# Moving output pairs of earlier batches into the load waits at the end of an attention and mixture-of-depths kernel

## The chip, the cores and the metric

The kernel runs on one core of a Trainium2 chip. The metric is the device time of one execution in microseconds; the kernel before takes 269.82 us (median of 3 runs, 269.68 to 270.16). The core has a matrix engine (TensorE, "PE" in the profile, its weight loads "PEld"), a vector engine (VectorE, "DVE"), an activation engine (ScalarE, "ACT"), a general one (GpSimd, "POOL") and one that here only issues stores (SyncE, "SP"). Loads, gathers and scatters are issued from GpSimd's queue, stores from SyncE's, and both are carried by the core's 16 DMA engines.

## The reference

Four batches; each q, k and v has 6208 rows of 256 channels. The attention is over channels: q and k are normalised over the rows, a 256 x 256 matrix is made of them, a softmax is taken along its rows, and v is multiplied by it. Then, in each batch, the 128 rows with the highest gate score go through a two-layer expert and are updated.

```python
def _attn_ref(q, k, v, tau):
    qn = q / (np.linalg.norm(q, axis=1, keepdims=True) + 1e-06)
    kn = k / (np.linalg.norm(k, axis=1, keepdims=True) + 1e-06)
    s = kn.transpose(0, 2, 1) @ qn / tau
    s = s - s.max(-1, keepdims=True)
    a = np.exp(s)
    a /= a.sum(-1, keepdims=True) + 1e-09
    return (v @ a).astype(np.float32)

def _moe_ref(x, w_gate, w1, w2, capacity):      # capacity 128, D 256, F 1024
    scores = np.einsum('bsd,d->bs', x, w_gate)
    out = x.copy()
    for b in range(B):
        top_idx = np.argpartition(-scores[b], capacity)[:capacity]
        xe = x[b, top_idx]
        ye = np.maximum(xe @ w1, 0.0) @ w2
        g = 1.0 / (1.0 + np.exp(-scores[b, top_idx]))
        out[b, top_idx] = x[b, top_idx] + g[:, None] * ye
    return out
```

## The kernel before

Rows are taken in chunks of 1024 (8 rows on each of 128 partitions): 6 full chunks and a remainder of 64 rows. A chunk is handled in two groups of 4 rows, so a batch has 13 groups, listed in `gs`; the last one is the remainder. For each group of v there are up to three kinds of work:

- `T`: 8 transposes of v on TensorE into a PSUM bank, and one copy to SBUF (`vt_sb`), on ScalarE where the flag is 1 and on VectorE where it is 0.
- `S`: gate scores, 8 matmuls that are two columns wide.
- `O`: output, two pairs of four 128x256 matmuls, each pair copied from PSUM to a staging buffer; a whole chunk is stored with one 1 MB transfer.

When all scores of a batch are there, `select_stages` finds the 128 best rows by a seven-step search of the threshold: each step compares and counts on VectorE, sums the counts over partitions with a small matmul, and goes on from the result. Then the rows of v are gathered, go through the expert (`mlp_stages`), and a scatter writes them over the stored rows. The scatter of a batch waits for that batch's stores.

The batches are numbered 0 to 3. In the code `L` is 3, the last one, `E` is 2 and `H` is 1. Batch 2 keeps most of its output (`rest`, from group 4 on) for the end, when there are no loads left. Batch 1 keeps the last chunk of its output, four "late pairs". They can't be written before the scatter, so their updated rows are added in the matmul itself, by one-hot matrices (`late_onehot`) times the expert's result in three bf16 parts:

```python
    def late_pair(k):
        g = late[k // 2]
        onehot, parts = late_moe
        ...
        o_ps = out_psum()
        row = g[1] + k % 2 * 2
        for pj in range(2):
            for cc in range(2):
                nc.tensor.matmul(o_ps[:, pj, :], lhsT=vts[(H, g)][:, cc, k % 2 * 2 + pj, :], rhs=a_sb[:, cc, :],
                                 start=pj == 0 and cc == 0, stop=False)
            for i in range(3):
                nc.tensor.matmul(o_ps[:, pj, :], lhsT=onehot[:, row + pj, :], rhs=parts[:, i, :],
                                 start=False, stop=pj == 1 and i == 2)
        nc.scalar.copy(st[:, row:row + 2, :], o_ps)
```

The plan of the tail, after the last q and k chunk. It stands in TensorE's program order:

```python
    rest = [("O", E, g, False) for g in gs[EARLY:]]        # EARLY = 4
    ...
    T = [("T", L, g, a) for g, a in zip(gs, [1, 1, 1, 0, 1, 1, 0, 1, 0, 1, 0, 1, 0])]
    S = [("S", L, g) for g in gs]
    plan += [("tail",)] + T[:2] + [("late", H, 0)] + T[2:4] + [("adv",), ("a", L)]
    plan += T[4:8] + [("late", H, 1)] + T[8:10] + S[:4] + [("warm", L, 4)] + T[10:] + [("side",)] + S[4:]
```

`("a", L)` finishes the last softmax, `("side",)` finishes the selection of batch 2, and `("warm", L, 4)` and `keep_warm(n)` issue matmuls whose results nobody reads:

```python
    def keep_warm(n):
        bank = ps_o.tile([P, 2, C], F32, name="o_ps")
        for _ in range(n):
            nc.tensor.matmul(bank[:, 0, 0:P], lhsT=ident_b, rhs=ones_b, start=True, stop=True)
```

After the plan, the last batch's selection starts, the stores held back so far ("deferred": 4 chunks) are issued behind the last but one v load, and the output phase follows:

```python
    b = B - 1
    side.append(select_stages(b))
    advance(side)
    advance(side)
    flush_deferred()
    ...
    now[0] = B + 1
    for op in rest:
        do_out(E, op[2], False)
    for i, g in enumerate(gs):
        do_out(b, g, False)
        if i in (8, 9):
            late_pair(i - 6)
    emit_store(H, NFULL - 1)
    while side:
        advance(side)
    while side2:
        advance_all(side2)
    while waiting:
        side2.append(mlp_stages(waiting.pop(0)))
    keep_warm(8)
    while side2:
        advance(side2)
```

In this phase every output pair calls `between()`, which puts the next step of the selection (and later of batch 2's expert) into the program after pairs 2, 4, 6, 8, 10, 13, 15, 18, 20 and so on. So TensorE takes up a step of the search only when it has done the pairs ahead of it:

```python
    def between():
        if now[0] > B:
            pairs[0] += 1
            due = pairs[0] in (2, 4, 6) or pairs[0] > 6 and pairs[0] % 5 in (0, 3)
            if due and not advance(side):
                advance_all(side2)
```

Line numbers that the profile shows: L402 transposes, L409 and L411 their copies, L430 scores, L476 output matmuls, L482 and L484 their copies, L500 and L503 the matmuls of a late pair, L505 its copy, L418 keep_warm, L561 to L636 the selection, L653 to L703 the expert, L535 the stores, L709 the scatter.

Of the kernel before, what the change touches and what calls it, by code (L numbers as in the profile page):

```python
# [26 lines left out]
def kernel(  # L27
# [70 lines left out]
    def groups(ci):  # L98
        return [(ci, 0, 4), (ci, 4, 4)] if ci < NFULL else [(ci, 0, 1)]

    gs = [g for ci in range(NFULL + 1) for g in groups(ci)]
    E = B - 2
    H = B - 3
    late = [(NFULL - 1, 0, 4), (NFULL - 1, 4, 4)]
# [18 lines left out]
    L = B - 1  # L123
    rest = [("O", E, g, False) for g in gs[EARLY:]]
    plan = []
# [17 lines left out]

    T = [("T", L, g, a) for g, a in zip(gs, [1, 1, 1, 0, 1, 1, 0, 1, 0, 1, 0, 1, 0])]
    S = [("S", L, g) for g in gs]
    plan += [("tail",)] + T[:2] + [("late", H, 0)] + T[2:4] + [("adv",), ("a", L)]
    plan += T[4:8] + [("late", H, 1)] + T[8:10] + S[:4] + [("warm", L, 4)] + T[10:] + [("side",)] + S[4:]
    units = []
    for op in plan:
        if op[0] in ("p1", "T"):  # L150
# [222 lines left out]
    side = []  # L373
# [40 lines left out]
# [5 lines that stand above are left out]
# [18 lines left out]
    def out_psum():  # L437

        if now[0] <= B:
            return ps_o.tile([P, 2, C], F32, name="o_ps")  # L440
        turn[0] += 1
        if turn[0] % 4 == 1:
            return ps_s.tile([P, 2, C], F32, name="s_ps")
        if turn[0] % 4 == 3:
            return ps_g.tile([P, 4, P], F32, name="g_ps").rearrange("p a c -> p (a c)").rearrange(
                "p (a c) -> p a c", a=2)
        return ps_o.tile([P, 2, C], F32, name="o_ps")
# [39 lines left out]
# [5 lines that stand above are left out]
        if k == 0:  # L492
            stage_of[(H, NFULL - 1)] = st_pool.tile([P, RPP, C], F32, name="stage")
        st = stage_of[(H, NFULL - 1)]
        a_sb = a_tiles[H][0]
# [10 lines that stand above are left out]
# [27 lines left out]
    def emit_store(b, ci):  # L533
        st = stage_of.pop((b, ci))
        ins = nc.sync.dma_start(out=view(out, b, ci), in_=st if ci < NFULL else st[:REM, 0, :])  # L535
        stores.append((b, ins))
        for o, sca in scatters:
            if o != b:
                tc.declare_no_dep(ins.ins, sca.ins, reason="rows of different batches")
        return ins  # L540
# [253 lines left out]
    def do_out(b, g, scores, defer=False):  # L794
        p2_out(b, g, vts.pop((b, g)), scores)
        if g[1] == 4 or g[0] == NFULL:
            held[b] -= 1
            if defer and now[0] <= B:
                deferred.append((b, g[0]))
            else:  # L800
                emit_store(b, g[0])
        spent((0.21 + (0.05 if scores else 0)) * g[2])
# [41 lines left out]
    while waiting:  # L844
        side2.append(mlp_stages(waiting.pop(0)))
    now[0] = B + 1
    for op in rest:
        do_out(E, op[2], False)
    for i, g in enumerate(gs):
        do_out(b, g, False)  # L850
        if i in (8, 9):
            late_pair(i - 6)
    emit_store(H, NFULL - 1)
    while side:
        advance(side)
# [1 line left out]
        advance_all(side2)  # L857
    while waiting:
        side2.append(mlp_stages(waiting.pop(0)))
    keep_warm(8)  # L860
    while side2:
        advance(side2)

# [34 lines left out]
```

## Time and profile before

| | before |
|---|---|
| time, median of 3 | 269.82 us |
| span of the profiled run | 269.3 us |
| PE busy | 205.6 us (76%) |
| DVE busy | 124.2 us (46%) |
| ACT busy | 80.7 us (30%) |
| bytes moved by DMA | 66.97 MB, mean 249 GB/s |
| stores from SyncE's queue | 24 of 1 MB, 4 of 64 KB |
| last q/k matmul ends | about 202.9 us |
| last v chunk taken up by TensorE | 216.24 us |
| last instruction that a compute engine's queue issues (scatter of batch 3) | 259.75 us |

Times are counted from the span's start. "Busy" is the time in which an engine executes; it says little here, since the kernel passes through stages with different limits. What counts is which wait ends last in the tail, from 203 us on. In rows of single instructions, the numbers are start and length, then engine, line, operation and tiles, and in brackets the idle time just before and what ended it. In the rows of slices, the busy time of each engine is followed by the clock that TensorE was granted (1.00 is full) and the share of time in which the DMA engines were busy.

### The profile page before, as it was taken

The numbers are of one execution on the slowest core, as the hardware profiler recorded it, in microseconds if no ns is written. First come the engines' busy times: TensorE is split into PE (matmuls) and PEld (weight loads), VectorE is DVE, ScalarE is ACT, GpSimd is POOL, SyncE is SP. The second block draws the span as 40 slices with busy tenths as digits, with TensorE's granted clock in tenths as the row PEclk, the third lists the DMA queues.
The fourth block names the chain that finished last, engine by engine and source line by source line (L and its number), as shares of the span: only waits on it lengthen the run. The fifth ranks groups of instructions, "written<-read, shape, count | busy, mean of one in ns | idle before, by whom it ended". The sixth has DMA issues, their size and how long they took to land.

```text
span 269.3 us, 6056 instructions
## 1 busy us (share of the span) xinstructions
PE 205.6 (76%) x2564; PEld 179.6 (67%) x2564; DVE 124.2 (46%) x476; ACT 80.7 (30%) x142; POOL 55.5 (21%) x104
## 2 busy tenths in 40 slices
PE   0197588899936877899978797899998578898820
PEld 0186577789925666789967686889996565587610
DVE  0200003624305376505457957765966537874510
ACT  2102000177710000147702001442107624775410
POOL 7113123211110023313002242211440011011010
PEclk9999899999968799599997999999999955999985
DMA  6999999999999999999999999999999996899960
GB/s 213 232 228 227 212 214 212 215 213 295 317 316 319 277 212 212 214 213 239 317 309 219 211 220 214 212 214 212 212 213 212 209 412 212 369 383 403 377 236 0
DMA packets 17642, 66.97 MB, mean 249 GB/s; under 512 B 2000, under 2 KB 4688, under 8 KB 14544
## 3 DMA queue, kind: packets, MB, share of 16 engines
q0 software_dynamic: 12384, 38.93, 72.4%
q1 hardware_dynamic: 5232, 27.66, 26.2%
q8 instruction: 20, 0.33, 0.4%
q14 instruction: 6, 0.05, 0.0%
HBM read 79.04 MB, written 25.95 MB: 390 GB/s over the span
## 4 chain that ended last, share of the span: by engine, by line
DMA 57%; PE 19%; issue 11%; DVE 7%; POOL 1%; ACT 1%; POOLq 1%; DVEq 0%
DMA k_ch<-in_k_dram 29%; DMA v_ch<-in_v_dram 17%; DMA q_ch<-in_q_dram 8%; PE o_ps L476 5%; PE s_ps L290 2%; DMA out_dram<-stage_rem 2%; PE vt_ps L402 2%; DVE cnt L590 1%; PE sc_ps L430 1%; PE s_ps L476 1%; DVE cmp L586 1%; PE g_ps L294 1%; PE g_ps L292 1%; PE g_ps L476 1%; PE o_ps L686 1%
## 5 line engine op out<-in xcount | busy, mean ns | idle before, releaser
L290 PE MATMUL s_ps<-q_ch,k_ch 128*128 128x256 bf16 x384 | 97.7, 293 | 29.3 <-DMA k_ch<-in_k_dram 28.5
L292 PE MATMUL g_ps<-q_ch 128*128 128x128 bf16 x384 | 89.1, 232 | 1.1 <-DVE nsq L309 1.0
L294 PE MATMUL g_ps<-k_ch 128*128 128x128 bf16 x384 | 89.1, 232 | 0.0
L290 PEld LDWEIGHTS <-k_ch 128*128 128x128 bf16 x384 | 40.3, 105 | 34.8 <-DMA k_ch<-in_k_dram 31.6
L294 PEld LDWEIGHTS <-k_ch 128*128 128x128 bf16 x384 | 40.3, 105 | 8.7 <-issue 1.6
L476 PE MATMUL o_ps<-a_sb,vt_sb 128*128 128x256 bf16 x294 | 44.9, 277 | 1.4 <-ACT vt_sb L409 1.3
L292 PEld LDWEIGHTS <-q_ch 128*128 128x128 bf16 x384 | 40.3, 105 | 1.2 <-issue 0.9
L484 ACT COPY stage<-o_ps 128x512 f32<-128x512 f32 x64 | 36.0, 588 | 16.0 <-PE o_ps L476 15.4
L476 PEld LDWEIGHTS <-vt_sb 128*128 128x128 bf16 (+1 forms) x376 | 30.8, 101 | 8.8 <-issue 3.9
L411 DVE COPY vt_sb<-vt_ps 128x1024 bf16<-128x1024 bf16 (+1 forms) x33 | 20.8, 634 | 32.2 <-PE vt_ps L402 32.1
L402 PEld LDWEIGHTS <-v_ch 128*128 128x128 bf16 x384 | 22.9, 99 | 6.4 <-DMA v_ch<-in_v_dram 5.3
L402 PE MATMUL vt_ps<-ident_b,v_ch 128*128 128x128 bf16 x336 | 24.6, 219 | 2.7 <-DMA v_ch<-in_v_dram 1.9
L430 PEld LDWEIGHTS <-vt_sb 128*128 128x128 bf16 (+1 forms) x376 | 24.0, 98 | 2.5 <-DVE u L553 0.2
L173 POOL DMA_DIRECT2D q_ch<-in_q_dram x23 | 12.7, 553 | 59.2 <-PE g_ps L294 36.3
L430 PE MATMUL sc_ps<-aw_sb,vt_sb 128*128 128x2 bf16 (+1 forms) x376 | 24.3, 164 | 0.0
L305 ACT COPY s_sb<-s_ps 128x512 f32<-128x512 f32 x4 | 2.3, 585 | 72.5 <-PE s_ps L290 42.7
L309 DVE CUSTOM_DVE_ANT_0 junk<-g_ps,ident_f 128x128 f32<-128x128 f32 x16 | 4.7, 291 | 39.1 <-PE g_ps L294 38.7
L173 POOL DMA_DIRECT2D v_ch<-in_v_dram x24 | 12.8, 538 | 24.4 <-DMA k_ch<-in_k_dram 11.5
L173 POOL DMA_DIRECT2D k_ch<-in_k_dram x23 | 12.5, 544 | 24.6 <-PE vt_ps L402 8.3
L409 ACT COPY vt_sb<-vt_ps 128x1024 bf16<-128x1024 bf16 x11 | 10.6, 1012 | 14.4 <-PE vt_ps L402 14.3
L590 DVE TENSOR_REDUCE cnt<-cmp 128x7 bf16<-128x343 bf16 x28 | 14.4, 513 | 1.0
L586 DVE SCALAR_TENSOR_TENSOR cmp<-u,delta,shares 128x343 bf16<-128x343 f32 x24 | 13.9, 578 | 0.9
(157 smaller groups left out, 219.5 us busy)
## 6 DMA issues: line engine op xcount, KB each, us to landing
out_dram<-stage SPq DMA_DIRECT2D x24, 1024.0 KB, 7.8
v_ch<-in_v_dram POOLq DMA_DIRECT2D x24, 512.0 KB, 14.8
q_ch<-in_q_dram POOLq DMA_DIRECT2D x23, 512.0 KB, 17.1
k_ch<-in_k_dram POOLq DMA_DIRECT2D x23, 512.0 KB, 17.2
stage<-in_moe_w_dram SPq DMA_DIRECT2D x2, 1024.0 KB, 5.3
q_ch<-in_q_dram POOLq DMA_DIRECT2D x2, 256.0 KB, 9.2
k_ch<-in_k_dram POOLq DMA_DIRECT2D x2, 256.0 KB, 9.2
out_dram<-stage_rem SPq DMA_DIRECT2D x4, 64.0 KB
```

Source lines behind the costliest of these rows:

```text
L173: ins = nc.gpsimd.dma_start(out=t, in_=view(src, b, ci))
L290: nc.tensor.matmul(s_ps[:, cc, :], lhsT=ks[:, sl], rhs=qs, start=first and cc == 0, stop=last and cc == 1)
L292: nc.tensor.matmul(g_ps[:, cc, :], lhsT=qs[:, sl], rhs=qs[:, sl], start=first and cc == 0, stop=False)
L294: nc.tensor.matmul(g_ps[:, 2 + cc, :], lhsT=ks[:, sl], rhs=ks[:, sl], start=False, stop=last and cc == 1)
L402: nc.tensor.transpose(vt_ps[:, cc, j, :parts], in_=vt[:parts, s0 + j, cc * P:(cc + 1) * P], identity=ident_b[:parts, :parts])
L409: nc.scalar.copy(vt_sb[:, :, :n, :parts], vt_ps[:, :, :n, :parts])
L411: nc.vector.tensor_copy(vt_sb[:, :, :n, :parts], vt_ps[:, :, :n, :parts])
L430: nc.tensor.matmul(sc_ps[:parts, col, :], lhsT=vt_sb[:, cc, j, :parts], rhs=aw_sb[:, cc, :], start=cc == 0 and col in (0, NCOL - 1), stop= ...
L476: nc.tensor.matmul(o_ps[:parts, pj, :], lhsT=vt_sb[:, cc, j, :parts], rhs=a_sb[:, cc, :], start=pj == 0 and cc == 0, stop=pj == m - 1 and ...
L484: nc.scalar.copy(st[:parts, s0 + pair * 2:s0 + pair * 2 + m, :], o_ps[:parts, :m, :])
L586: nc.vector.scalar_tensor_tensor(out=cmp, in0=wide, scalar=delta, in1=thr, op0=ALU.subtract, op1=ALU.is_ge)
L590: nc.vector.tensor_reduce(out=cnt, in_=cmp, axis=AX.X, op=ALU.add)
```

## The change

It reorders the tail. All four late pairs stand between the last transposes, where TensorE waits for v (two of them stood there before, two in the output phase). The first kept output group of batch 2 (two pairs) is computed before the last scores of batch 3, and six score groups instead of four stand ahead of the last three transposes; the four keep-warm matmuls in that place go. The remainder of the last batch, a 64 KB store, is computed and stored ahead of its full chunks. The keep-warm run ahead of the last expert has 24 matmuls in place of 8. Nothing that is loaded, stored or computed for the result is added or taken away.

```diff
     T = [("T", L, g, a) for g, a in zip(gs, [1, 1, 1, 0, 1, 1, 0, 1, 0, 1, 0, 1, 0])]
     S = [("S", L, g) for g in gs]
-    plan += [("tail",)] + T[:2] + [("late", H, 0)] + T[2:4] + [("adv",), ("a", L)]
-    plan += T[4:8] + [("late", H, 1)] + T[8:10] + S[:4] + [("warm", L, 4)] + T[10:] + [("side",)] + S[4:]
+    W = [("late", H, k) for k in range(4)]
+    plan += [("tail",)] + T[:2] + W[:1] + T[2:4] + [("adv",), ("a", L)] + T[4:6] + W[1:2] + T[6:8] + W[2:]
+    plan += T[8:10] + S[:6] + T[10:] + rest[:1] + [("side",)] + S[6:]
...
     now[0] = B + 1
-    for op in rest:
+    for op in rest[1:]:
         do_out(E, op[2], False)
-    for i, g in enumerate(gs):
+    for g in gs[-1:] + gs[:-1]:
         do_out(b, g, False)
-        if i in (8, 9):
-            late_pair(i - 6)
     emit_store(H, NFULL - 1)
...
-    keep_warm(8)
+    keep_warm(24)
     while side2:
         advance(side2)
```

## The prediction

> **What bounds the kernel now.** I read the page first, for where the end comes from, then the chain that ended last, then the tail in slices of 2 us, then the tail's instructions one by one. The diff touches only what stands after the last q and k load, so only the stretch from about 203 us to the end can change. The page's sum of the chain:
>
> ```profile
> DMA 57%; PE 19%; issue 11%; DVE 7%; POOL 1%; ACT 1%; POOLq 1%; DVEq 0%
> ```
>
> Over the whole span the loads rule, and the change leaves every load as it is. In the tail the chain is another. Its last rows (start, length, what):
>
> ```profile
> 222.62 0.29 DVE lo L568
> ...
> 252.96 0.61 PE o_ps L418 x8
> 253.57 0.12 PE vt_ps L653 x2
> 253.69 5.15 DMA out_dram<-stage_rem
> 258.99 0.54 issue
> 259.53 1.19 POOLq L893
> ```
>
> From 222 to 253 us it runs through TensorE and VectorE (the search of the last batch's threshold, mixed with output pairs), then through the last batch's 64 KB remainder store, then to the last scatter on GpSimd. The instructions around it show how close a second chain is:
>
> ```profile
> 258.07 0.48 DVE L703 SCALAR_TENSOR_TENSOR upd<-o_ps,gate,xe 128x256 f32<-128x256 f32 x1 [1.52 <-PE o_ps L694]
> 259.75 0.97 POOL L709 DMA_INDIRECT out_dram<-upd,idx  x1 [11.03 <-DMA out_dram<-stage_rem]
> ```
>
> The scatter needs two things: the last batch's stores landed (258.99) and its update rows (`upd`, done at 258.07 + 0.48 = 258.55). They come within half a microsecond of each other, so **both** must become earlier. After the scatter's issue the rest is fixed: 269.3 - 259.75 = 9.55 us, which I carry over.
>
> The slices show what the transfers do (columns: busy time of PE, PEld, DVE, ACT, POOL, then granted clock, DMA share, GB/s):
>
> ```profile
> 212.00:214.00 2.00, 0.61 (x8) 0.32 (x7) 0.00 (x0) 0.96 (x2) 0.00 (x0) 1.00 0.74 142
> 214.00:216.00 2.00, 1.90 (x52) 1.72 (x49) 0.69 (x1) 1.01 (x1) 0.00 (x0) 0.97 0.92 329
> 216.00:218.00 2.00, 1.76 (x16) 1.62 (x16) 0.69 (x1) 0.00 (x0) 0.00 (x0) 0.50 1.00 410
> ...
> 226.00:228.00 2.00, 2.00 (x12) 1.39 (x11) 1.65 (x6) 1.17 (x2) 0.00 (x0) 0.50 0.06 15
> 228.00:230.00 2.00, 2.00 (x14) 1.49 (x12) 1.67 (x6) 1.43 (x3) 0.00 (x0) 0.61 0.79 328
> 230.00:232.00 2.00, 1.29 (x13) 0.89 (x11) 1.83 (x7) 1.84 (x4) 0.00 (x0) 1.00 0.66 270
> ...
> 246.00:248.00 2.00, 2.00 (x21) 1.79 (x20) 1.38 (x3) 0.69 (x2) 0.26 (x1) 1.00 1.01 426
> ```
>
> Stores alone move 410 to 438 GB/s. At 226 to 228 us they move 15: the four deferred stores are out, and batch 2's next chunk is not written yet (its store issues at 227.78). TensorE's clock is 0.50 from about 215.8 to 229.2. The TensorE rows say why the outputs are late:
>
> ```profile
> 213.81 1.07 PE L402 MATMUL vt_ps<-ident_b,v_ch 128*128 128x128 bf16 x16 [1.39 <-DMA v_ch<-in_v_dram]
> ...
> 216.24 1.03 PE L402 MATMUL s_ps<-ident_b,v_ch 128*128 128x128 bf16 x8 [0.34 <-DMA v_ch<-in_v_dram]
> ...
> 218.32 2.05 PE L430 MATMUL sc_ps<-aw_sb,vt_sb 128*128 128x2 bf16 x66
> 221.82 0.77 PE L561 MATMUL m_ps<-ident_f,mx 128*128 128x128 f32 x2 [1.45 <-DVE mx L558]
> 222.38 1.06 PE L476 MATMUL s_ps<-a_sb,vt_sb 128*128 128x256 bf16 x4
> ```
>
> TensorE waits 1.4 us for v twice (before 210.26 and 213.81) and 0.5 before 207.79; after the last load (216.24) 66 scores still follow, at half clock, before the threshold search (first step at 221.12) and the first output pair (222.38) can begin.
>
> **What the Trainium skill says.** (1) *TensorE: Matmul & The Clock Gate*, Part 1: the array runs at half clock after a mostly idle window of about 3.4 us and at full clock after a busy one. The trace agrees: four 128x256 matmuls start 0.85 us apart at 222.38/223.23 (clock 0.50) and 0.44 apart at 230.34/230.78 (clock 1.00), and the drop follows the 212 to 214 slice with 0.61 us of work. (2) *DMA: Bandwidth & Descriptors*, "Queues, rings and completion order": a DMA engine takes the descriptors of one ring in order. It fits the 64 KB remainder store taking 5.15 us: it stands behind a 1 MB store. (3) Same page, "Anatomy of one DMA": the completion signal comes some time after the last byte. The trace lumps that into the 5.15 us.
>
> **The change, part by part.**
>
> *Late pairs 2 and 3 into the load waits.* One late pair costs TensorE 1.09 us (211.16 to 212.25). Two leave the output phase, where TensorE is back to back (2.00 busy of 2 us at 248 to 252): -2.18 us there. They go to 211.16-213.35, where TensorE now does one pair and idles 1.39 us; pair 1 moves up to 208.7. All fits before v lands at 213.8: cost 0.
>
> *Fuller waits keep the clock.* With W2, W3 and 48 scores before 216.24 instead of 32 scores and 4 keep-warm matmuls, I expect clock 1.00 at 216. Then from the landing: 18 transposes 1.01 us (16 take 0.90 at 213.81-214.71), two output pairs of batch 2 0.88, `side` about 0.04, 50 scores at 25 ns (32 in 0.80) 1.25: sum 3.2, so scores end at about 219.5 and the first search step is at 219.6 instead of 221.12: **-1.5 us**. At half clock it would be 5.8 us and a loss of about 1.
>
> *From the first search step to the last output pair.* Now 252.96 - 221.12 = 31.84. Off: the two late pairs, 2.18, and the two full output pairs of batch 2 that now stand ahead of `side`, 2 x 0.44 = 0.88 (42 pairs follow the first search step now, 40 then). Off for the clock: the f32 matmul 0.2, and three search steps at half clock 1.70 instead of 1.59, 0.3. So 31.84 - 2.18 - 0.88 - 0.5 = 28.3, and the last pair ends at 219.6 + 28.3 = 247.9. The search itself does not shrink: each step is 1.59 us of VectorE with its matmul (L597 at 230.32, 231.91, 233.50), whatever TensorE does.
>
> *keep_warm 8 to 24.* 16 more matmuls at 55 ns (8 in 0.44 at 252.96-253.40): +0.88, directly in the last chain.
>
> *Last batch's expert.* 258.55 - 252.96 = 5.59, unchanged. `upd` at 247.9 + 0.88 + 5.59 = 254.4; scatter 0.28 later (batch 2's: `upd` 247.46, scatter 247.74): **254.7** by this chain.
>
> *Stores.* Remaining at 214: 15.86 MB on the store queue. The deferred four are out at about 225. Batch 2's chunk 2 is now ready at about 222.5 (two pairs already done, two right after 220.3, ACT 0.6), chunk 3 at 226.6, then one per 3.2 us or faster, so the gap at 226 to 228 closes. From 225: 4 + 6 MB-stores and two remainders at 2.5 to 2.6 us per store (1.049 MB at 410 to 426 GB/s) is 25.3 to 26.3, plus about 0.5 of small gaps and gathers: batch 3's last chunk is through at 251 to 252. In the kernel before, the remainder's signal came about 1.7 us after its byte's turn in the queue (by my count of the trace's transfer records), so landed at about 253 to 253.7, and the scatter 0.76 later (258.99 to 259.75): **253.8 to 254.5**. Batch 1's held store now stands behind it and no longer matters to the scatter; moving the remainder to the front removes a 64 KB store that waited in last place.
>
> The later of two nearly equal ends, with their scatter, gives 255.0. Then 255.0 + 9.55 = 264.5 on the profile, 4.75 us less than 269.3; from the median 269.82 that is **265.0 us**, 1.8% faster.
>
> **Rivals.** (a) *The clock drops anyway.* Scores are two columns wide and may not count as work; the stretch 219.5 to 222.6 holds only about 1.4 us of matmuls. For it: the drop at 215.8 came although 32 scores had just run. Against: the new order has 256-column output pairs there, and the pattern at 230 to 236, 0.88 us of pairs per 1.59, kept 1.00. If the drop is after 222: +0.4 us (265.4). If at 216 already: +2.5 (267.5). (b) *The store queue is the bound.* If stores run at 2.7 us each, as the last two did by the same count, batch 3's chunk 5 lands 1 to 1.5 us later and the end is 266. (c) *The extra keep_warm is wasted or hides*: if stores end last, it costs nothing; if the expert chain does, its 0.88 is all loss. (d) *ScalarE becomes late*: it gets two more late copies (0.59 each) beside transposes' copies of 1.01, but in 208 to 216 it is busy 5.3 of 8 us, so 1.2 us more fit.
>
> **Range and chances.** Everything well: 263.5 (clock held, stores at 2.5, expert chain 1 us shorter). Both rivals (a) late and (b): 267. The 2% line is 264.42, 0.6 under my value with a spread of about 1: chance of over 2% faster 0.31, of within 2% 0.66, slower 0.03, as nothing in the change adds load or store bytes.
>
> **What would show it.** Clock 1.00 from 211 to 222; scores' end and first reduce near 219.6; batch 2's first new store at 222 to 223 and no slice under 0.7 DMA share between 224 and 232; late-pair rows only before 213.5; search steps still 1.59 apart; last pair at 248; `upd` at 254.4; scatter at 255. The prediction is wrong if the first reduce stays near 221 (clock), if the scatter waits for the stores after 255.5 (queue), or if the 9.55 us after the scatter change.

## The result, and the profile after

The changed kernel takes **267.76 us** (median of 4 runs, 267.18 to 267.99) against 269.99 for the kernel before in the same session; the ratio is 0.9912 with a 95% interval of 0.989 to 0.9935. A later comparison with 22 runs of it and 55 of the kernel before gave 0.9956 (0.9936 to 0.9976). So it is about 0.4 to 0.9% faster by the two comparisons. The prediction said 265.0 us, with 263.5 to 267.0 as its range: the gain was predicted more than twice as large as it is.

The end of the chain that ended last, in the changed kernel (start, length, what; line numbers from L144 on are one or two off those of the kernel before):

```profile
247.45 0.45 PE o_ps L477 x4
247.92 0.70 DVE stage L483
248.68 6.36 DMA out_dram<-stage
255.20 0.54 issue
255.73 1.19 POOLq L892
```

The last output pair ends at 247.9. Then the chain no longer goes on through a 64 KB remainder but through the 1 MB store of batch 3's last chunk, which needs 6.36 us from issue to landing. The expert's chain of the changed kernel, in the timeline of single instructions, still ends beside it:

```profile
254.59 0.48 DVE L704 SCALAR_TENSOR_TENSOR upd<-o_ps,gate,xe 128x256 f32<-128x256 f32 x1 [2.31 <-PE o_ps L695]
255.96 0.97 POOL L710 DMA_INDIRECT out_dram<-upd,idx  x1 [9.35 <-DVE upd L704]
```

`upd` is done at 255.07, the store landed at 255.04, the scatter is issued at 255.96. The bracket names `upd`, which came last by 0.03 us; which of the two holds the scatter can't be read here, and experiments below settle it.

The TensorE rows around the last loads, changed kernel:

```profile
213.44 1.07 PE L403 MATMUL vt_ps<-ident_b,v_ch 128*128 128x128 bf16 x16
214.35 1.34 PE L431 MATMUL sc_ps<-aw_sb,vt_sb 128*128 128x2 bf16 x48
215.55 0.61 PE L403 MATMUL s_ps<-ident_b,v_ch 128*128 128x128 bf16 x8
...
217.62 1.49 PE L431 MATMUL sc_ps<-aw_sb,vt_sb 128*128 128x2 bf16 x50
219.84 0.46 PE L562 MATMUL m_ps<-ident_f,mx 128*128 128x128 f32 x2 [0.74 <-DVE mx L559]
220.14 0.60 PE L477 MATMUL s_ps<-a_sb,vt_sb 128*128 128x256 bf16 x4
```

From 213 us on no row waits for v, and the first pair of the output phase starts at 220.14 in place of 222.38. The slices (busy PE, PEld, DVE, ACT, POOL, then clock, DMA share, GB/s):

```profile
212.00:214.00 2.00, 1.94 (x23) 1.55 (x22) 0.00 (x0) 1.41 (x3) 0.00 (x0) 1.00 0.70 135
216.00:218.00 2.00, 2.00 (x38) 1.75 (x36) 0.99 (x3) 1.35 (x2) 0.00 (x0) 1.00 0.97 401
...
222.00:224.00 2.00, 1.00 (x6) 0.74 (x6) 1.67 (x5) 0.00 (x0) 0.47 (x1) 0.50 1.05 406
...
226.00:228.00 2.00, 2.00 (x12) 1.44 (x11) 1.68 (x7) 1.44 (x3) 0.00 (x0) 0.50 0.87 362
...
230.00:232.00 2.00, 1.91 (x18) 1.38 (x17) 1.76 (x8) 1.69 (x4) 0.00 (x0) 1.00 0.85 352
...
236.00:238.00 2.00, 2.00 (x22) 1.80 (x20) 1.33 (x6) 1.70 (x4) 0.97 (x1) 1.00 0.83 310
238.00:240.00 2.00, 2.00 (x21) 1.80 (x20) 2.00 (x5) 1.17 (x2) 0.00 (x0) 1.00 0.83 308
```

The waits are filled (1.94 us of TensorE in 212 to 214, 0.61 before), the clock is 1.00 at 216, and the hole in the transfers at 226 to 228 is nearly gone (share 0.87, before 0.06). That hole was the first profile's, though: in the third profile of the kernel before, which comes below, the same slice has 0.95, and the lowest share after it is 0.65, at 228 to 230. Smaller holes stand in the changed kernel at 230 to 232 and at 236 to 240. The clock falls after all, from 221.9 to 228.7.

### The profile page after: what moved, and what is told of

Read it like the earlier page. It is cut to its first block, busy times and chain, and to the rows that moved or that the text cites. A ratio compares the mean times of both kernels' runs of the same rounds, so it can differ in the third digit from the quotient of the medians.

```text
span 265.5 us, 6081 instructions
## 1 busy us (share of the span) xinstructions
PE 203.3 (77%) x2576; PEld 178.1 (67%) x2576; DVE 123.7 (47%) x475; ACT 80.9 (30%) x143; POOL 55.6 (21%) x104
## 4 chain that ended last, share of the span: by engine, by line
DMA 57%; PE 19%; issue 11%; DVE 7%; POOL 1%; ACT 1%; POOLq 1%; DVEq 0%; SPq 0%
DMA k_ch<-in_k_dram 25%; DMA v_ch<-in_v_dram 17%; DMA q_ch<-in_q_dram 13%; PE o_ps L477 6%; DMA out_dram<-stage 2%; PE s_ps L291 2%; PE vt_ps L403 2%; PE sc_ps L431 1%; PE g_ps L477 1%; PE s_ps L477 1%; DVE cnt L591 1%; PE g_ps L295 1%; PE g_ps L293 1%; DVE cmp L587 1%; DVE stage L483 1%
## 5 line engine op out<-in xcount | busy, mean ns | idle before, releaser
L291 PE MATMUL s_ps<-q_ch,k_ch 128*128 128x256 bf16 x384 | 96.3, 290 | 30.5 <-DMA k_ch<-in_k_dram 29.8
L291 PEld LDWEIGHTS <-k_ch 128*128 128x128 bf16 x384 | 39.9, 104 | 36.2 <-DMA k_ch<-in_k_dram 33.2
L295 PEld LDWEIGHTS <-k_ch 128*128 128x128 bf16 x384 | 39.9, 104 | 8.3 <-issue 1.6
L403 PEld LDWEIGHTS <-v_ch 128*128 128x128 bf16 x384 | 22.2, 97 | 3.6 <-DMA v_ch<-in_v_dram 2.5
```

Of the source, the lines that this page charges most:

```text
L291: nc.tensor.matmul(s_ps[:, cc, :], lhsT=ks[:, sl], rhs=qs, start=first and cc == 0, stop=last and cc == 1)
L295: nc.tensor.matmul(g_ps[:, 2 + cc, :], lhsT=ks[:, sl], rhs=ks[:, sl], start=False, stop=last and cc == 1)
L403: nc.tensor.transpose(vt_ps[:, cc, j, :parts], in_=vt[:parts, s0 + j, cc * P:(cc + 1) * P], identity=ident_b[:parts, :parts])
```

## The experiments

Times are compared with the kernel before in the same session, on which the medians are 269.07 to 269.24, and 270.0 in the last session. All edits are to the changed kernel unless it says "to the kernel before".

### The changed kernel and the kernel before once more

> The changed kernel unchanged, to see how far one profiled run stands from another. Theory A (the base of the prediction was off: the profiled run of the kernel before, 269.3 us of span, was about 1 us longer than its own median): this one is 0.991 of the kernel before, its span is 265.5 to 266.5, and the kernel before has spans near 268.3. Rival B (the tail of the change itself varies by 1 to 2 us from run to run): the time from the first store's issue to the last scatter's issue, 42.5 us in the first profile, is 43.5 or more here.

Ratio 0.9956 (0.9936 to 0.9976), span 265.6 us. First held-back store issued at 213.46, last scatter at 256.05: a tail of 42.6 us, in the first profile 213.41 to 255.96, 42.55. The changed kernel's tail repeats itself. Here `upd` is done at 254.39 and the store lands at 255.14, and the scatter comes no earlier. The expected ratio of 0.991 was missed. Both profiled runs of the changed kernel, of 267.18 and 267.27 us, lie 0.5 to 0.6 us under its medians (267.76 and 267.79).

> The kernel before, unchanged, for a second profile. Theory A (the profile that the prediction was built on was a long one of its kind: 270.97 us for the run that it was taken from, the median is 269.2 to 270.0): the span is 267 to 268.5, and the time from the first held-back store's issue (213.78 in the first profile) to the last scatter's issue (259.75) is 0.7 to 1.8 us shorter than the 46.0 us of the first. Rival: it is 46 again, and then the changed kernel's 42.5 us tail is a real 3.4 us shorter and the rest of the span took it back.

> The kernel before once more, for one more profile, beside the first two (270.97 and 270.42 us, both over the median of 269.1 to 269.4). If its time is near the median, theory A says where the extra 1 to 1.5 us of the first two stood: in the tail between the first store's issue and the last scatter's (44 to 45 us here against 45.7 and 46.0). If it is near 270.5 too, nothing is learnt of that.

The second profile was of a run of 270.42 us, with a tail of 45.7 us and the clock at half from 215.9 on, as in the first: by itself it supported the rival. The third is of a run of 269.06 us, at the median, and its tail is 213.45 to 257.84, **44.4 us**, against 213.78 to 259.75, 46.0, in the profile that the prediction was built on. The first reduce of the threshold search, in the first and then in the third profile of the same kernel:

```profile
221.12 0.26 DVE L554 TENSOR_REDUCE sc<-sc_ps 128x48 f32<-128x96 f32 x1 [1.60 <-PE sc_ps L430]
```

```profile
219.00 0.26 DVE L554 TENSOR_REDUCE sc<-sc_ps 128x48 f32<-128x96 f32 x1 [0.74 <-PE sc_ps L430]
```

And the slices of the third profile of the kernel before:

```profile
210.00:212.00 2.00, 1.68 (x17) 1.68 (x18) 1.81 (x6) 0.77 (x1) 0.00 (x0) 0.63 1.04 212
212.00:214.00 2.00, 2.00 (x12) 1.42 (x11) 0.00 (x0) 1.01 (x1) 0.00 (x0) 0.52 0.68 130
...
216.00:218.00 2.00, 2.00 (x57) 1.85 (x55) 1.36 (x7) 1.09 (x2) 0.00 (x0) 1.00 0.96 397
218.00:220.00 2.00, 1.26 (x37) 1.18 (x34) 0.78 (x6) 0.00 (x0) 1.00 (x1) 1.00 1.05 438
...
222.00:224.00 2.00, 1.15 (x7) 0.84 (x7) 1.64 (x6) 0.07 (x1) 0.71 (x1) 0.50 1.01 377
```

Here the clock falls at 210.5, where TensorE has time to spare, is back at 213.9, stays full over the last transposes and scores, and falls again at 220.8. In the first profile it fell at 215.9 and came back at 229.5, over exactly the part that counts. The time between two changes of the clock is 3.4 us or a multiple of it in all these profiles. *TensorE: Matmul & The Clock Gate*, Part 1, in the Trainium skill, calls this window free-running: it does not reset when a kernel starts. That fits one program with two courses of the clock; that the window's position is the cause wasn't tried. So the changed kernel's first reduce at 219.15 is 2 us ahead of one run of the kernel before and level with another. The tail goes with the clock: it is 45.7 and 46.0 us where the clock is at half from 216 to 218 us, and 44.4 us here, where it is full. The runs with the remainder first (44.15 us) and with keep-warm matmuls in the waits (44.0 us), both below and both at full clock from 216 to 218, agree.

### The clock without the late pairs

To the kernel before:

```diff
-    plan += T[4:8] + [("late", H, 1)] + T[8:10] + S[:4] + [("warm", L, 4)] + T[10:] + [("side",)] + S[4:]
+    plan += T[4:6] + [("warm", L, 20)] + T[6:8] + [("late", H, 1), ("warm", L, 20)]
+    plan += T[8:10] + S[:4] + [("warm", L, 4)] + T[10:] + [("side",)] + S[4:]
```

> The kernel before with 20 keep-warm matmuls (1.1 us) in each of the two load waits that the change fills with late pairs; the late pairs and everything else stay where they were. Theory B (the 1.5 us for an earlier first reduce was never the change's to gain in a usual run: whether the clock falls at 215.9, as in the profile that the prediction used, or at 210.5 and again at 220.8, as in the third profile, hangs on where the clock's 3.4 us steps fall): clock 1.00 up to about 220, first reduce at 219.0 to 219.5, as in the third profile of the kernel before (219.00), and the median of the time stays within 0.4 us of the kernel before, since only its longest runs are shortened. Rival: the half clock is what most runs of the kernel before pay, and holding it up alone brings 1 us or more.

Ratio 0.998 (0.9959 to 1.0001), 269.33 against 270.0 us. The clock holds to 219.9; the first reduce is at 219.95, later than expected, and the last scatter at 257.54. Filling the waits with work that nobody needs brings about 0.5 us by the ratio (0 to 1.1 by the interval, so the rival's 1 us is only at its edge; the expected 0.4 was slightly exceeded), and not the 2.0 us (1.5 for the reduce, 0.5 for the rest) that the prediction gave to the clock. Long runs remain: three of the 14 here take over 270 us, and five of the 22 of the changed kernel take 269.6 to 270.4 where the others stay under 268.4. None of these was profiled, so what lengthens them is open.

### Single parts of the change, each alone on the kernel before

Late pairs alone (the plan's lines as in the change but with `S[:4]`, `("warm", L, 4)` and no `rest[:1]`; the two `late_pair` calls of the output phase go):

> The kernel before with one part of the change: all four late pairs in the load waits, none in the output phase; the 4 keep-warm matmuls, the order of the scores, of batch 2 and of the remainder and the 8 keep-warm matmuls at the end as before. Theory Q (once batch 3's chunk 0 is handed over, the store queue is never empty again, so the last landing follows the issue of that chunk's store; two pairs taken out after it only help where the queue ran dry near the end): clock 1.00 to about 219, first reduce at 219.5 to 220.5, and a gain of 0.5 to 1.3 us. Rival P (TensorE's sum of work is the bound, as the prediction had it): 2.2 us and more from the late pairs alone.

0.9978 (0.9952 to 1.0004), 268.60 against 269.07 us. First reduce at 219.13, batch 3's chunk 0 stored from 236.91, last scatter at 257.40. Rival P's 2.2 us are excluded. 2.2 us of matmuls left the output phase for about 0.5 us of time, which is not clear of nothing (0 to 1.3) and no more than keep-warm matmuls in the same waits brought.

The first kept group of batch 2 ahead of the last scores (with `S[:6]`, and without the 4 keep-warm matmuls):

> The kernel before with another part: the first kept group of batch 2 ahead of the last scores, six score groups ahead of the last transposes, no 4 keep-warm matmuls; two late pairs still in the output phase, remainder last, 8 keep-warm matmuls at the end. Theory Q: batch 2's chunk 2 is stored 3 to 5 us earlier, so the hole at 226 to 228 closes, but chunk 0 of batch 3 comes at most 0.9 us earlier (two pairs fewer in a stretch paced by the search), so 0 to 0.6 us in the end, as closing a hole far ahead of the last one gains nothing. Rival H (every hole of the queue counts in the sum): 1.5 to 2 us.

0.998 (0.9961 to 0.9999), 268.58 us: 0 to 1.1 us, so rival H is excluded. Batch 2's chunk 2 is stored from 224.0 in place of 227.8 in the first profile of the kernel before, and the hole doesn't close, it moves:

```profile
226.00:228.00 2.00, 2.00 (x12) 1.45 (x11) 1.66 (x6) 1.44 (x3) 0.00 (x0) 0.50 0.92 385
228.00:230.00 2.00, 2.00 (x13) 1.34 (x12) 1.69 (x7) 1.44 (x3) 0.00 (x0) 0.61 0.06 25
```

The next chunk is stored only from 229.18, so the queue is empty two microseconds later instead. This profile's run was itself 1.4 us over its median, with the clock at half from 215.9 to 219.3; that it is as deep at full clock is not shown.

The remainder first, late pairs after the same chunks as before:

> The kernel before with one part of the change: the last batch's remainder first, the late pairs after the same chunks as before, all else as before. The scatter then waits for the last full chunk in place of the remainder behind it; batch 1's held store stays last. Theory Q: the remainder's store lands almost together with the chunk ahead of it, so 0 to 0.3 us. Rival (a small store in last place costs its own completion time): 0.5 to 1 us faster.

1.0011 (0.999 to 1.0032): nothing. The scatter now waits for the 1 MB chunk, issued at 251.33, and is issued at 257.81; with the remainder last it was 257.84. A small store in last place cost nothing, since it landed with the big one ahead of it (issued at 250.88 and 251.30 in the third profile, landed 5.9 and 5.6 us later).

The late pairs and the first kept group come to 0.22 and 0.20%, the whole change to 0.44% by the comparison of that kind. With intervals of 0.2 to 0.3% on each side, that the parts add up is not shown.

### What the last scatter waits for

```diff
-    keep_warm(24)
+    keep_warm(8)
```

> The changed kernel with 8 keep-warm matmuls ahead of the last expert in place of 24. Theory S (the last scatter waits for batch 3's last 1 MB store, landed at 255.0; the expert's rows at 255.07 only happen to come together with it): upd is 0.9 to 1.7 us earlier, the scatter stays near 255.5 to 256, the time is within 0.3 us of the changed kernel's. Theory X (the expert's chain alone holds the scatter, and the stores' landing would follow): 0.9 to 1.7 us faster, ratio to the changed kernel about 0.995.

0.9962 (0.9938 to 0.9985), 267.95 us: no different from the changed kernel. Its last instructions:

```profile
252.98 0.48 DVE L704 SCALAR_TENSOR_TENSOR upd<-o_ps,gate,xe 128x256 f32<-128x256 f32 x1 [1.53 <-PE o_ps L695]
256.74 0.97 POOL L710 DMA_INDIRECT out_dram<-upd,idx  x1 [10.06 <-DMA out_dram<-stage]
```

The expert's rows are ready 1.6 us earlier (253.46), and the scatter doesn't come earlier at all. **The stores hold it**, not the expert: the last 1 MB store, issued at 248.75, needed 7.08 us here. The extra keep-warm matmuls are hidden.

Next, one store less (the output of that chunk is not written):

```diff
         st = stage_of.pop((b, ci))
+        if (b, ci) == (E, NFULL - 1):
+            return None
```

> The changed kernel without the store of batch 2's last full chunk (1 MB of output isn't written). One store costs 2.5 us of the queue. Theory S with both ends nearly equal: the last chunk lands 1 to 2.5 us earlier, but the expert's rows at about 255.1 hold the scatter at 255.3 to 255.6, so the gain is 0.3 to 0.7 us. If the stores alone hold it: 2 us or more. If the expert alone: 0.

> Both of the above: 8 keep-warm matmuls and one store less. Theory S with both ends nearly equal: upd at 253.4 to 254.2 and the landing at 252.6 to 254, so the scatter is 1 to 2 us earlier than in the changed kernel, more than the sum of the two alone. If one of the two ends alone holds the scatter, this gains no more than the better of the two.

0.9956 (0.9928 to 0.9985) and 0.9947 (0.9933 to 0.996), last scatters at 256.60 and 256.10. Neither differs from the changed kernel's 0.9956 beyond the noise. A megabyte less changed nothing, alone or with the shorter keep-warm run: the expected gains were missed. The slices of the first show where the megabyte went:

```profile
232.00:236.00 4.00, 3.28 (x30) 2.15 (x28) 2.97 (x14) 3.17 (x8) 0.00 (x0) 1.00 0.52 199
236.00:240.00 4.00, 4.00 (x40) 3.60 (x41) 3.13 (x11) 3.17 (x7) 0.97 (x1) 1.00 0.71 279
```

The transfers simply idled for that long. The changed kernel itself shows where its queue last runs short, in slices of half a microsecond:

```profile
236.50:237.00 0.50, 0.50 (x8) 0.46 (x6) 0.20 (x1) 0.50 (x2) 0.03 (x1) 1.00 0.35 98
239.50:240.00 0.50, 0.50 (x8) 0.45 (x6) 0.50 (x2) 0.20 (x1) 0.00 (x0) 1.00 0.38 62
```

These are the two sides of batch 3's chunk 0, whose store is issued at 236.17; from 240 until the last chunk lands at 255.04 the share of no such slice is under 0.8. So batch 2's megabytes have run out before chunk 0 and 1 move, and one of them more or less doesn't count. What counts is when batch 3's chunks come. From the issue of chunk 0's store to the landing of the last chunk it takes 18.87 us in both profiles of the changed kernel, 18.99 and 18.83 with the store left out, and 19.6 in the run with 8 keep-warm matmuls and all stores, where the last store itself was slow.

### The pace of the output phase

```diff
-            due = pairs[0] in (2, 4, 6) or pairs[0] > 6 and pairs[0] % 5 in (0, 3)
+            due = pairs[0] % 3 == 0
```

> The changed kernel with a step of the selection after every third output pair in place of every second (3, 6, 9 and so on). Theory Q: chunk 0 of batch 3 is ready 2 to 4 us earlier, the store queue stays full from 214 on, and the last landing and the scatter come 1 to 2 us earlier than in the changed kernel (time 265.8 to 266.8), though the search ends later. Rival (the transfers already move as fast as they can, or the expert's rows at the end take over): within 0.3 us of the changed kernel.

**0.9907 (0.988 to 0.9934), median 266.37 us**, the best version here. Now three pairs (1.3 us) stand between two steps of the search (1.59 us). The slices:

```profile
224.00:228.00 4.00, 3.85 (x36) 3.16 (x34) 3.62 (x12) 3.80 (x9) 0.00 (x0) 1.00 1.07 406
228.00:232.00 4.00, 3.60 (x30) 2.37 (x29) 3.52 (x15) 3.65 (x8) 0.00 (x0) 1.00 1.02 426
232.00:236.00 4.00, 3.90 (x40) 3.34 (x39) 2.69 (x13) 3.88 (x9) 0.00 (x0) 1.00 0.97 379
236.00:240.00 4.00, 4.00 (x40) 3.61 (x38) 2.81 (x10) 3.50 (x8) 0.96 (x1) 1.00 1.04 424
```

No hole like those is left. The remainder of batch 3 is stored from 231.78, and chunk 0 from 233.54, 2.6 us earlier than in the changed kernel. The rows of chunk 0's store, in the changed kernel and here (where a second store follows at once):

```profile
236.17 0.34 SPq L536 DMA_DIRECT2D out_dram<-stage  x1
```

```profile
233.54 2.16 SPq L536 DMA_DIRECT2D out_dram<-stage  x2
```

The last scatter is issued at 254.87, 1.1 us earlier. Why not more, its waits on GpSimd's queue say:

```profile
POOL out_dram L710 <- DMA out_dram<-upd,idx: 8.0, 1, 8.0
```

The last scatter waits for batch 2's scatter, issued at 245.90 into the full queue and landed at 254.07. Without that wait it could hardly have come sooner: batch 3's last store, issued at 244.61, took 9.3 us and so landed at 253.9. From 224 to 254 us no slice of 2 us has a share under 0.94, so here the transfers have next to no idle time left to give.

> The kernel with a selection step after every third pair, without the store of batch 2's last full chunk (1 MB isn't written). In the changed kernel the same omission gained nothing, as the queue ran dry behind it. Theory Q: here the queue is full from 214 us to the end, so every megabyte counts: the last landing comes 1.5 to 2.5 us earlier and the time is 264 to 265, unless the wait for batch 2's scatter or the expert's rows (upd at about 251.4) end later. Rival (another wait sets the end there too): within 0.3 us of 266.4.

Inconclusive: 0.9906 (0.9871 to 0.9941), median 267.18 of 6 runs from 265.24 to 267.68, no gain shown over the version above. In the profile, batch 3's softmax (ScalarE's first copy) starts 3.5 us later than in the changed kernel. This experiment first, the changed kernel second:

```profile
206.27 0.59 ACT L306 COPY s_sb<-s_ps 128x512 f32<-128x512 f32 x1 [10.22 <-PE s_ps L291]
```

```profile
202.76 0.59 ACT L306 COPY s_sb<-s_ps 128x512 f32<-128x512 f32 x1 [10.80 <-PE s_ps L291]
```

So its tail can't be compared by the clock. Within it, the premise failed:

```profile
234.00:236.00 2.00, 1.90 (x19) 1.56 (x18) 1.75 (x8) 1.94 (x4) 0.00 (x0) 1.00 0.28 84
```

The queue ran dry again where the megabyte was missing, just ahead of chunk 0's store (235.13). The last scatter waited for batch 2's again (247.87 to 255.21), 1.5 us longer than for the last store, landed at 253.7. Whether bytes or that wait bound the three-pair version stays open.

### The clock in the output phase

```diff
             due = pairs[0] in (2, 4, 6) or pairs[0] > 6 and pairs[0] % 5 in (0, 3)
+            if pairs[0] == 2:
+                keep_warm(28)
```

> The changed kernel with 28 keep-warm matmuls (about 1.5 us) in the wait of TensorE after the second output pair, where it has nothing to do for 1.8 us. Theory C (that gap is why the clock falls to 0.50 from 222 to 229, and the slower search steps, 1.73 in place of 1.59 us, delay batch 3's chunk 0): clock 1.00 through 220 to 236, chunk 0's store issued 0.5 to 0.8 us earlier, and by theory Q the scatter and the time by the same 0.5 to 0.8 us. Rival: the clock falls all the same, or holds and the time doesn't move, since the search is paced by VectorE.

0.9963 (0.9939 to 0.9988). The clock does hold, where it was 0.50 from 221.9 to 228.7:

```profile
220.00:224.00 4.00, 3.67 (x46) 3.41 (x47) 2.97 (x11) 1.19 (x3) 1.30 (x2) 1.00 1.02 401
224.00:228.00 4.00, 2.40 (x22) 1.70 (x20) 3.62 (x13) 2.96 (x6) 0.00 (x0) 1.00 1.06 396
```

From the first to the seventh count of the search (the rows of L598 and of the line that answers to it) 9.55 us pass in place of 10.01. But chunk 0 is stored from 235.93 in place of 236.17, the last scatter is issued at 255.70 in place of 255.96, and the times show no gain. The expected 0.5 to 0.8 us didn't come. A step of the search takes 1.59 us at full clock, where the profile shows no wait of VectorE, and 1.73 at half clock, where it waits about 0.26 us for the small matmul. So the half clock costs the search about 0.46 us in all, and about 0.3 us is what the profile shows at the end.

## Why the prediction was wrong, point by point

**The base of the sum was off.** The prediction worked out what the tail of one profile would lose, 4.75 us, and took that off the median of 269.82. But the profile's run took 270.97 us, 1.15 more than the median. Its tail was 46.0 us, and in the profile at the median it is 44.4. The terms that failed are "the first search step is at 219.6 instead of 221.12: -1.5 us" and the 0.5 us for the clock after it. The 219.6 was right (219.15, then 219.40). The 221.12 was one course of the clock, not the kernel's: in the third profile it is 219.00. And the 0.5 us was not gained, since the clock is at half for 6.8 us of the output phase in that profile and in the changed kernel alike. The prediction even named the cause, the clock at 0.50 from 215.8 (in the profile 215.9 to 229.5), and took it for a property of the program.

**The stores of the changed kernel ended later.** The prediction had the span at 264.5 us; it was 265.5 in a run of 267.18. From the first held-back store to the last scatter it had 255.0 - 213.78 = 41.2 us (its later chain ended at 254.7; for the 0.3 us more it gives no reason), and 42.55 was measured, begun 0.4 us earlier. The failing term is "about 0.5 of small gaps and gathers" in the stores, with the last chunk landed at 253 to 253.7. It landed at 255.04. The shares in the slices at 226, 230, 236 and 238 alone add up to 2 x (0.13 + 0.15 + 0.17 + 0.17) = 1.2 us of idle transfers. GpSimd's queue, with batch 3's gather and batch 2's scatter, took time as well, between 236 and 253.3 us of the changed kernel (packets, MB, share of the 16 engines' time):

```profile
q0 software_dynamic: 192, 0.20, 5.6%
```

That is 5.6% of 17.3 us, 1.0 us. Batch 2's chunk 3 was stored from 227.28 (predicted 226.6), and batch 3's chunk 0 from 236.17, 3.5 us after chunk 5 of batch 2, so the queue ran short late, where nothing behind it could catch up. The experiment with three pairs for each search step shows that these idle stretches count: with them gone the scatter came 1.1 us earlier. The one with a store left out shows that a stretch ahead of the last of them doesn't. The prediction's own sign for this, a scatter that waits for the stores after 255.5, came true (255.96).

**The account.** Of the 2.7 us between 265.07 and 267.76, 1.15 are the base, about 0.95 the later end of the span (265.5 for 264.55), and 0.6 that this profile's run lay under its own median.

**What held.** The last pair was predicted at 247.9 and ended at 247.9, with some luck: the first reduce came 0.45 us early (0.4 of it the loads), and from there to the last pair it took 28.75 us in place of 28.3. The late pairs fitted into the waits at no cost. Batch 2's chunk 2 was stored at 221.88 (predicted 222 to 223), the search steps at full clock stayed 1.59 us apart, 9.55 us followed the scatter (9.54), and the clock was 1.00 from 211 to 221.9. That the clock would fall afterwards was rival (a), and its cost of 0.4 us was of the right size (about 0.3 at the end).

**What held and didn't matter.** `upd` came 0.7 us later than predicted (255.07, and 0.4 of loads earlier besides): the clock fell at 252.6 in that run and the last eight matmuls took 1.89 us in place of 1.10. The run with 8 keep-warm matmuls shows that all of it was hidden: rival (c), first half. Rival (b), the store queue as the bound with the last chunk 1 to 1.5 us later, was right in kind and size; but its mechanism, 2.7 us per store, was not. In the slices from 244 to 254 the transfers moved 412 to 430 GB/s, about 2.5 us per store: the queue was short of chunks, and shared with a gather and a scatter, but not slow.

**Credit for parts.** The prediction took off 2.18 us for the two late pairs and 0.88 for the two output pairs as if TensorE's sum set the end. Alone they brought about 0.5 us each, hardly more than the noise, and the remainder's new place nothing. Most of the TensorE time they free lies beside the store queue.

## What to carry to other kernels

Before a gain is taken off a profile, compare that run's own time with the median, and see whether the clock's course in a second profile is the same: a stretch at half clock may belong to the run and not to the program. Where stores end last, ask for the last moment at which the queue runs dry; only what brings the chunk after it forward moved the end here, and a megabyte ahead of it was free. Where two chains end together, shorten each alone: the one whose shortening does nothing wasn't the bound.

## What was not expected of the hardware

- Two profiles of one program showed the clock at half from 215.9 to 229.5, and from 210.5 to 213.9 and 220.8 to 227.6. Every length is about 3.4 us or a multiple of it: 13.7, 3.4 and 6.8 us.
- 24 keep-warm matmuls just ahead of the last expert didn't always keep the clock: it fell at 252.6, within the expert, in the first profile of the changed kernel, and only at 258.7, after the last matmul, in the second.
- A 128-row scatter issued into a full store queue took 8.2 us to land (245.90 to 254.07 in the three-pair version; 4.8 in the changed kernel), so that a later scatter waited for it.
